# Memory retrieval from the transposed queries: row-tiled matmuls on [M | z], the division after the matmul, and a new order of the attention steps

## The chip, the core and the metric

One core of a Trainium2 chip runs the whole kernel. The metric is the device time of one execution in microseconds; lower is better. The engines are named as in the profile: PE is TensorE's matmul stream and PEld its weight loads, DVE is VectorE, ACT is ScalarE, POOL is GpSimd, SP issues most of the DMAs.

## The reference

Attention with a compressed memory over B = 4 batches, H = 8 heads, S = 576 tokens, D = 64, followed by two feed-forward layers on the 2304 x 512 result:

```python
scores = scale * np.matmul(q, k.transpose(0, 1, 3, 2))      # causal, softmax -> a
local = np.matmul(a, v)
q_p = phi(q)                                                # elu(q) + 1
mem_ret = np.einsum('bhsd,bhde->bhse', q_p, M_prev)
mem_norm = np.einsum('bhsd,bhd->bhs', q_p, z_prev)[..., None] + 1e-06
g = 1.0 / (1.0 + np.exp(-beta))[None, :, None, None]
attn = g * mem_ret / mem_norm + (1 - g) * local
...
h = x @ w_in;  y = (h * np.cos(h)) @ w_out                  # first layer
r = np.maximum(y @ w2_in, 0);  out = (r * r) @ w2_out       # second layer
```

The `moe_` and `moe2_` weights come as 64-bit floats and are turned into fp32, and from there into a high and a low fp32r part, on the chip.

## The kernel before

**Attention.** The work is cut into 16 units, one for each batch and pair of heads. The two heads of a pair stand on partitions 0 to 63 and 64 to 127 of the transposed operands, so a matmul with 64 rows of one head can run beside that of the other. For a unit u the steps are: `S0` to `S3` (scores, fp32, into the PSUM pool `ps_s` of two buffers), `R0` to `R3` (DVE: mask, scale and row minimum out of PSUM), `E0` to `E3` (ACT: exp with row sums), `Ns0`, `Ns1` (DVE: reciprocals with the gate), `Np0` to `Np3` (POOL: normalise the probabilities), `PT0` to `PT6` (PE transposes of the probabilities into the pool `ps_t` of two buffers), `V0` to `V6` (copies of these into SBUF, by ACT or DVE as the string `pt` says), `PV0` to `PV4` (probabilities times v, into the one accumulator `O_t`), `mem` (memory part added into `O_t`), `X` (ACT copies `O_t` out, a DMA stores it as a slice of `xT`).

**Memory retrieval before.** `q1` to `q3` make phi(q) from q in row form (`qr`, a load of its own, 320 KB per unit). `q4` (POOL) multiplies it by z, broadcast over 128 partitions by a DMA (`zb`); `q5` (DVE) sums it over d and takes the reciprocal with the gate; `q6` (POOL) multiplies phi(q) by that; `qpT` transposes the product on PE and `qpV` copies it out on ACT; `mem` multiplies it with a block-diagonal M (128 x 128, `mbd`), 512 and 64 columns wide, into `O_t`.

**Conversion of weights.** `c1` to `c9` carry one weight tile per unit through the 64-bit conversion: `c1` absolute value (ACT), `c2` clamp (DVE here), `c3`, `c4`, `c6` (DVE), `c5` (ACT), then for the first 8 units the high and low split (`c8` ACT, `c9` POOL), for the last 8 a store.

**Order.** `CFG['order']` is a list of step/offset pairs, run once for each u from -2 on; `S1/2` in round u is the step S1 of unit u+2. Each engine runs its steps of the list in this order (the `_Pinned` wrapper chains them), so one late step holds all behind it on its engine. SP issues the DMAs in order too: in a round the loads of unit u+2 (line 720 on), then `xT`, the v load after `PV3`, and the next weight tile. Buffers: `qk` (transposed q and k, 640 KB) and `qr` two each, `vr` three, raw weights two.

**End of attention.** `CFG['fill']` puts the first three steps of the feed-forward part (`l` = its matmuls, `a` to `g` = its elementwise chain) into the slots of units that no longer exist. The feed-forward part itself (`moe`) is not pinned: the tile framework places its instructions where its own schedule finds room, inside the last rounds of attention too. In the trace its lines bear their own numbers (L157 to L169, L256), those of attention L47 or L44.

Of the kernel before, what the change touches and what calls it, by code (L numbers as in the profile page):

```python
# [32 lines left out]
class _Pinned:  # L33
# [23 lines left out]
    S0/1 c5/1 R1/1 PT0/0 PT1/0 X/-2 E1/1 q5/0 S2/1 PV0/-1 R0/1 R2/1 V1/0 PV2/-1 PV1/-1 q1/1 V0/0  # L57
    c1/0 PV4/-1 q6/0 PV3/-1 PT2/0 E0/1 q2/1 PT4/0 c2/0 Ns0/1 S3/1 mem/-1 c3/0 c4/0 Np2/0 V2/0 R3/1
    PT3/0 qpT/0 Np0/1 q3/1 E2/1 V4/0 c6/0 PT6/0 V3/0 PT5/0 qpV/0 Np1/1 V5/0 V6/0 S1/2 E3/1 q4/1
    Ns1/1 c8/0 c9/0 Np3/1  # L60
""",
       'pt': 'AAAAADD',
       'norm': 'PPPP',
       'qpt': 'A',
# [20 lines left out]
def kernel(  # L85
# [14 lines left out]
    nc = tc.nc  # L100
# [48 lines left out]
    def c_steps(raw, clamp=None, rest=None):  # L149
# [6 lines left out]
        return af, [  # L156
            lambda: act.activation(out=af, in_=hi.bitcast(F32), func=AF.Abs),  # L157
            lambda: (clamp or pool).tensor_scalar(
                out=af, in0=af, scalar1=MAG_MAX, scalar2=MAG_MIN, op0=ALU.min, op1=ALU.max
            ),  # L160
            lambda: dve.tensor_scalar(
                out=a, in0=a, scalar1=3, scalar2=0x3FFFFFF8,
                op0=ALU.logical_shift_left, op1=ALU.bitwise_and,
            ),
            lambda: dve.scalar_tensor_tensor(  # L165
                out=b, in0=hi, scalar=-0x40000000, in1=a, op0=ALU.bitwise_and, op1=ALU.bitwise_or
            ),
            lambda: act.activation(out=r, in_=lo.bitcast(U32), func=AF.Copy, scale=2.0 ** -29),
            lambda: dve.tensor_tensor(out=a, in0=b, in1=r, op=ALU.add),  # L169
        ]  # L170
# [153 lines left out]
    def attention(ctx):  # L324
# [14 lines left out]
        mbd = [ac.tile([128, NP, 128], F32, name=f"mbd{i}") for i in range(2)]  # L339
# [11 lines left out]
        def load(u, first=False):  # L351
            b, p = divmod(u, NP)
            t = ae.tile([128, 2 * S + 128], F32, tag="qk", name="qk")
            if first:
                nc.scalar.dma_start(out=t[:, S:2 * S], in_=qk[b, p, :, S:2 * S])
                nc.sync.dma_start(out=t[:, 0:S], in_=qk[b, p, :, 0:S])
                nc.scalar.dma_start(out=t[:, 2 * S:], in_=qk[b, p, :, 2 * S:])
            else:
                nc.sync.dma_start(out=t, in_=qk[b, p])
            raw["qk", u] = t  # L360
            t = ae.tile([128, NKT, 2, D], F32, tag="qr", name="qr")
            nc.sync.dma_start(out=t, in_=qrow[b, p])
            raw["q", u] = t
            t = ae.tile([128, 2, D], F32, tag="zb", name="zb", bufs=3)
            nc.sync.dma_start(
                out=t.rearrange("p h d -> p (h d)"),
                in_=z_prev[b:b + 1, 2 * p:2 * p + 2].rearrange("o h d -> o (h d)").partition_broadcast(128),
            )
            raw["z", u] = t
# [7 lines left out]
        def load_mem(b):  # L377
            m = mbd[b % 2]
            for h in range(2):
                nc.sync.dma_start(  # L380
                    out=m[h * 64:(h + 1) * 64, :, h * 64:(h + 1) * 64],
                    in_=M_prev[b].rearrange("(p two) d e -> two d p e", two=2)[h],
                )

        qp_t = {}

        ee = {}

        def q1(u):
            qr = raw["q", u].rearrange("p t h d -> p (t h d)")  # L390
            ee[u] = ae.tile([128, NKT * 2, D], F32, tag="e", name="e", bufs=1)
            ef = ee[u].rearrange("p a d -> p (a d)")
            dve.tensor_scalar(out=ef, in0=qr, scalar1=0.0, scalar2=None, op0=ALU.min)

        def q2(u):
            ef = ee[u].rearrange("p a d -> p (a d)")
            act.activation(out=ef, in_=ef, func=AF.Exp)

        def q3(u):
            qr = raw["q", u].rearrange("p t h d -> p (t h d)")  # L400
            qp_t[u] = ae.tile([128, NKT * 2, D], F32, tag="qp", name="qp")
            dve.scalar_tensor_tensor(
                out=qp_t[u].rearrange("p a d -> p (a d)"), in0=qr, scalar=0.0,
                in1=ee[u].rearrange("p a d -> p (a d)"), op0=ALU.max, op1=ALU.add,
            )

        def q4(u):
            zz = raw["z", u].rearrange("p h d -> p (h d)")
            pool.tensor_tensor(
                out=ee[u].rearrange("p (t h) d -> p t (h d)", h=2),  # L410
                in0=qp_t[u].rearrange("p (t h) d -> p t (h d)", h=2),
                in1=zz.unsqueeze(1).to_broadcast([128, NKT, 2 * D]),
                op=ALU.mult,
            )
# [15 lines left out]
        def q6(u):  # L430
            mnf = mns.pop(u).rearrange("p t h -> p (t h)")
            pool.tensor_tensor(
                out=qp_t[u], in0=qp_t[u], in1=mnf.unsqueeze(2).to_broadcast([128, NKT * 2, D]),
                op=ALU.mult,
            )

        qpT = {}

        def emit_qpT(u):
            qp = qp_t.pop(u)  # L440
            ps = ps_s.tile([128, 2, 512], F32, tag="s", name="qps").rearrange("p a b -> p (a b)")
            for t in range(NKT):
                w = KW[t]
                pe.transpose(
                    out=ps[:, t * 128:t * 128 + w],
                    in_=qp[0:w, 2 * t:2 * t + 2, :].rearrange("p h d -> p (h d)"),
                    identity=ident[0:w, 0:w],
                )
            qpT[u] = ps
# [145 lines left out]
        def emit_mem(u):  # L595
            b, p = divmod(u, NP)
            for a, e in ((0, 512), (512, S)):
                pe.matmul(
                    out=O_t[u][:, a:e],
                    lhsT=mbd[b % 2][:, p, :],  # L600
                    rhs=qpT[u][:, a:e],
                    start=False,
                    stop=True,
                    skip_group_check=True,
                )
# [56 lines left out]
        for t in mbd:  # L662
# [24 lines left out]
        def conv_load(n):  # L687
            if todo and 0 <= n < NU:
                what, kd, f = todo.pop()
                tiles[n] = [what, kd, f, *c_steps(c_load(wsrc[kd, 1], kd, f), dve, a2)]  # L690

        def conv(n, x):
            what, kd, f, wf, ops = tiles[n][:5]
            if x <= 6:
                if x == 5 and n == 0:
                    return
                if x == 2 and n == 0:
# [15 lines left out]
            "q1": q1, "q2": q2, "q3": q3, "q4": q4, "q5": q5, "q6": q6,  # L713
            "qpT": emit_qpT, "qpV": emit_qpV, "mem": emit_mem, "X": emit_X,
# [3 lines left out]
        XL, xraws = CFG["xl"], []  # L718
        for u in range(first, end):
# [10 lines left out]
            for t, d in program:  # L730
# [6 lines left out]
                if 0 <= u + d < NU:  # L737
                    if t == "Ns0" and u + d == 0:
                        gates()
# [180 lines left out]
_INS = ['M_prev', 'z_prev', 'beta', 'moe_w_in', 'moe_w_out', 'moe2_w_in', 'moe2_w_out']  # L920
# [3 lines left out]
def _layout(np, q, k, v):  # L924
# [16 lines left out]
    return {"qk": qk, "qrow": rows(q), "vrow": rows(v)}  # L941
# [28 lines left out]
```

## Time and profile before

| | |
|---|---|
| median of 3 runs | 1047.77 us (1046.26 to 1050.31) |
| the profiled execution | 1047.47 us, span 1045.7 us |
| busy over the span | PE 96%, PEld 76%, DVE 58%, ACT 54%, POOL 28% |
| chain that ended last, by engine | PE 71%, DVE 10%, DMA 8%, ACT 7% |

The busy shares mix two parts: attention, up to about 228 us, in which all engines work, and the feed-forward part, in which PE does nearly everything. Attention has to be read by itself.

### The profile page before, as it was taken

The page shows a single profiled execution, that of the slowest core. Times are in us where ns is not written, and L with a number is a line of the kernel's source. Part 1 is how long each engine was busy: PE and PEld are TensorE (multiplying, and loading weights), DVE is VectorE, ACT ScalarE, POOL GpSimd, SP SyncE. Part 2 cuts the span into 40 slices and gives each one's busy share as a digit, 9 for nine tenths or more (in the row PEclk, how much of TensorE's full clock was granted, in tenths as well). Part 3 has the DMA queues.
Part 4 walks back from the last instruction along what each step waited for, and adds up shares of the span by engine and source line. Part 5 has one row for each costly group of instructions (what it writes and reads, how often), then busy time and mean ns, then how long its engine had stood idle before and what let it go on. Part 6 is the DMA issues. An engine that isn't in the chain of part 4 may idle for free.

```text
span 1045.7 us, 14485 instructions
## 1 busy us (share of the span) xinstructions
PE 1005.4 (96%) x5200; PEld 796.0 (76%) x5200; DVE 603.2 (58%) x1235; ACT 567.6 (54%) x1152; POOL 288.9 (28%) x306
## 2 busy tenths in 40 slices
PE   6999999879899999999999999999999999999998
PEld 4666666657687778788998778788888888888887
DVE  5999999648777878555555589623222322322232
ACT  5999999757776766445556667423222322322222
POOL 5999888637432110000003544300000000000000
PEclk8999999989999999999999999999999999999999
DMA  7565666144425664100103324201100200000010
GB/s 213 178 209 195 217 210 216 66 134 140 141 81 155 188 208 155 41 1 20 61 21 110 112 82 135 87 1 41 41 1 1 71 1 1 21 31 1 0 42 21
DMA packets 56873, 95.33 MB, mean 91 GB/s; under 512 B 8032, under 2 KB 29920, under 8 KB 56800
## 3 DMA queue, kind: packets, MB, share of 16 engines
q1 hardware_dynamic: 56224, 93.90, 28.0%
q8 instruction: 41, 0.67, 0.3%
q10 hardware_dynamic: 576, 0.50, 0.1%
q14 instruction: 32, 0.26, 0.1%
HBM read 72.88 MB, written 21.50 MB: 90 GB/s over the span
## 4 chain that ended last, share of the span: by engine, by line
PE 71%; DVE 10%; DMA 8%; ACT 7%; issue 3%; POOL 2%; SPq 0%; POOLq 0%; DVEq 0%; ACTq 0%
PE a L772 29%; PE h L256 28%; PE o L47 5%; PE ptps L47 3%; PE sps L47 3%; DMA wraw<-in_moe_w_out_dram 2%; DVE wa L169 1%; DVE wb L165 1%; DMA wf<-ws2in 1%; DMA xraw<-xT 1%; DVE gf L289 1%; DMA ws2out<-wa 1%; PE h L47 1%; DMA wf<-ws2out 1%; DMA ws2in<-wa 1%
## 5 line engine op out<-in xcount | busy, mean ns | idle before, releaser
L256 PE MATMUL h<-xh,winh 128*128 128x512 f32 (+1 forms) x628 | 234.0, 373 | 3.6 <-DVE gf L302 1.7
L256 PE MATMUL h<-xl,winh 128*128 128x512 f32 (+1 forms) x628 | 233.6, 372 | 0.0
L256 PE MATMUL h<-xh,winl 128*128 128x512 f32 (+1 forms) x628 | 233.1, 371 | 0.0
L314 DVE TENSOR_TENSOR gl<-gf,gh 128x512 fp32r<-128x512 f32 (+1 forms) x156 | 104.5, 670 | 130.0 <-ACT gh L307 129.8
L307 ACT ACTIVATE gh<-gf 128x512 fp32r<-128x512 f32 (+1 forms) x158 | 92.2, 584 | 113.6 <-PE a L772 96.1
L256 PEld LDWEIGHTS h<-xh,winh 128*128 128x128 f32 x628 | 118.2, 188 | 28.6 <-DVE gf L302 3.3
L256 PEld LDWEIGHTS h<-xh,winl 128*128 128x128 f32 x628 | 118.3, 188 | 22.4
L256 PEld LDWEIGHTS h<-xl,winh 128*128 128x128 f32 x628 | 118.2, 188 | 22.4
L285 DVE TENSOR_TENSOR gf<-gf 128x512 f32<-128x512 f32 (+1 forms) x80 | 51.9, 653 | 134.7 <-ACT gf L277 134.5
L277 ACT ACTIVATE gf<-h 128x512 f32<-128x512 f32 (+1 forms) x80 | 43.9, 554 | 152.0 <-PE h L256 151.1
L772 PE MATMUL a<-gl,wouth 128*128 128x512 f32 (+1 forms) x320 | 118.0, 375 | 0.6 <-DVE gl L314 0.5
L772 PE MATMUL a<-gh,woutl 128*128 128x512 f32 (+1 forms) x320 | 117.8, 374 | 0.0
L772 PE MATMUL a<-woutl,gh 128*128 128x512 f32 x288 | 112.9, 392 | 0.0
L772 PE MATMUL a<-wouth,gl 128*128 128x512 f32 x288 | 112.9, 392 | 0.0
L47 POOL TENSOR_SCALAR P<-P,sm 128x512 f32<-128x512 f32 (+3 forms) x128 | 97.4, 779 | 13.1 <-DVE sm L47 11.9
L772 PE MATMUL a<-wouth,gh 128*128 128x512 f32 x288 | 99.1, 393 | 1.1 <-ACT gh L307 1.1
L772 PE MATMUL a<-gh,wouth 128*128 128x512 f32 (+1 forms) x320 | 85.9, 375 | 8.2 <-ACT gh L307 7.3
L302 DVE TENSOR_TENSOR gf<-h,gf 128x512 f32<-128x512 f32 (+1 forms) x78 | 49.4, 634 | 60.4 <-PE h L256 43.7
L772 PEld LDWEIGHTS a<-gh,wouth 128*128 128x128 f32 x320 | 56.4, 188 | 22.8 <-ACT gh L307 11.0
L275 ACT ACTIVATE ki<-h 128x512 int32<-128x512 f32 (+1 forms) x77 | 42.2, 548 | 57.9 <-DVE gf L302 49.0
L47 PE MATMUL sps<-qk 64*128 64x384 f32 (+4 forms) x320 | 63.1, 455 | 8.7 <-DMA qk<-in_qk_dram 4.6
L772 PEld LDWEIGHTS a<-gl,wouth 128*128 128x128 f32 x320 | 61.0, 191 | 12.4 <-DVE gl L314 1.4
(113 smaller groups left out, 1631.9 us busy)
## 6 DMA issues: line engine op xcount, KB each, us to landing
wraw<-in_moe_w_in_dram SPq DMA_DIRECT2D x32, 512.0 KB, 3.9
wraw<-in_moe_w_out_dram SPq DMA_DIRECT2D x32, 512.0 KB, 3.7
qk<-in_qk_dram SPq DMA_DIRECT2D x15, 640.0 KB, 5.1
qr<-in_qrow_dram SPq DMA_DIRECT2D x16, 320.0 KB, 4.6
vr<-in_vrow_dram SPq DMA_DIRECT2D x16, 320.0 KB, 2.9
xT<-x SPq DMA_DIRECT2D x16, 288.0 KB, 3.1
out_dram<-ob SPq DMA_DIRECT2D x17, 256.0 KB, 2.3
x1T<-ob SPq DMA_DIRECT2D x16, 256.0 KB, 2.6
```

The costliest lines, as they stand in the source:

```text
L47: made = call(*args, **kwargs)
L165: lambda: dve.scalar_tensor_tensor(out=b, in0=hi, scalar=-0x40000000, in1=a, op0=ALU.bitwise_and, op1=ALU.bitwise_or),
L169: lambda: dve.tensor_tensor(out=a, in0=b, in1=r, op=ALU.add),
L256: pe.matmul(out=h[:, 0:n], lhsT=lt[:, kk * 128:(kk + 1) * 128], rhs=rt[:, 0:n], start=(kk == 0 and x == 0), stop=(kk == KD - 1 and x == 2),)
L275: act.activation(out=kis[s], in_=hs[s], func=AF.Copy, scale=1.0 / TWO_PI)
L277: act.activation(out=rs[s], in_=hs[s], func=AF.Relu)
L285: dve.tensor_tensor(out=rs[s], in0=rs[s], in1=rs[s], op=ALU.mult)
L289: dve.scalar_tensor_tensor(out=rs[s], in0=kis[s], scalar=-C2, in1=rs[s], op0=ALU.mult, op1=ALU.add)
L302: dve.tensor_tensor(out=rs[s], in0=hs[s], in1=rs[s], op=ALU.mult)
L307: act.activation(out=gh, in_=rs[s], func=AF.Copy)
L314: eng.tensor_tensor(out=gl, in0=rs[s], in1=gs[s].bitcast(F32), op=ALU.subtract)
L772: nc.tensor.matmul(out=o, lhsT=lt, rhs=rt, start=((p, j, f) in opens and x == 0), stop=((p, j, f) in closes and x == 2),)
```

## The change

The memory part starts from the transposed q, which is already there in `qk`. `q1` to `q3` work on 576 columns of it and write phi(q) transposed into `qpb`. A new step `qm` multiplies, for each of the five blocks of 128 tokens and each head, 64 rows of phi(q) (stationary) with [M | z] of that head (64 x 65, moving): the product has the 64 retrieved columns and the norm in column 65, both heads in their own PSUM bank. `q4` (DVE) takes norm, gate and reciprocal from PSUM, `q5` (DVE) multiplies the retrieved columns by it on their way to SBUF (`mr`), and `mem` becomes five accumulating transposes of `mr` into `O_t`. The loads `qr` and `zb` go; a small load `zcol` comes. `q4` and `q6` on POOL, `qpT` and `qpV` go. `c1` moves from ACT to DVE, `c2` from DVE to POOL, `V3` from ACT to DVE. The order is new; `mem` now runs two rounds late, and for the last two units `mem` and `X` follow the last `PV` at once. The first M and v loads come later.

```diff
-    S0/1 c5/1 R1/1 PT0/0 PT1/0 X/-2 E1/1 q5/0 S2/1 PV0/-1 R0/1 R2/1 V1/0 PV2/-1 PV1/-1 q1/1 V0/0
-    c1/0 PV4/-1 q6/0 PV3/-1 PT2/0 E0/1 q2/1 PT4/0 c2/0 Ns0/1 S3/1 mem/-1 c3/0 c4/0 Np2/0 V2/0 R3/1
-    PT3/0 qpT/0 Np0/1 q3/1 E2/1 V4/0 c6/0 PT6/0 V3/0 PT5/0 qpV/0 Np1/1 V5/0 V6/0 S1/2 E3/1 q4/1
-    Ns1/1 c8/0 c9/0 Np3/1
+    V6/-1 Np3/0 c5/1 c2/0 c8/-1 S0/1 S2/1 q1/1 PT1/0 R0/1 PT0/0 R2/1 E1/1 q2/1 Np2/0 S3/1 V1/0 PT2/0
+    V0/0 c3/0 mem/-2 PT3/0 c4/0 R3/1 qm/0 E0/1 S1/2 V3/0 V2/0 E3/1 Ns0/1 PT4/0 X/-2 PT5/0 c6/0 PV0/-1
+    PV3/-1 q3/1 q4/0 V5/0 q5/0 c9/-1 E2/1 V4/0 Np1/1 Np0/1 Ns1/1 c1/1 PV2/-1 R1/2 PV4/-1 PV1/-1 PT6/0
-       'pt': 'AAAAADD',
+       'pt': 'AAADADD',
+       'abs': 'D',
+       'clamp': 'P',
...
+            dve.tensor_scalar(out=a, in0=hi, scalar1=0x7FFFFFFF, scalar2=None, op0=ALU.bitwise_and)
...
-        mbd = [ac.tile([128, NP, 128], F32, name=f"mbd{i}") for i in range(2)]
+        mbd = [ac.tile([128, NP, 65], F32, name=f"mbd{i}") for i in range(2)]
+        qpb = [a2.tile([128, 640], F32, name=f"qp{i}", bufs=1) for i in range(2)]
...
-            nc.sync.dma_start(out=t, in_=qrow[b, p])
...
+            nc.sync.dma_start(out=m[:, :, 64:65], in_=zcol[b])
...
+        def qm(u):
+            b, p = divmod(u, NP)
+            ps = mem_ps[u] = ps_s.tile([128, 2, 512], F32, tag="s", name="qps")
+            for t in range(NKT):
+                for h in range(2):
+                    r = slice(64 * h, 64 * h + 64)
+                    pe.matmul(
+                        out=ps[:, h, 65 * t:65 * t + 65],
+                        lhsT=qpb[u % 2][r, 128 * t:128 * t + 128],
+                        rhs=mbd[b % 2][r, p, :],
+                        start=True, stop=True,
+                    )
...
+        def q5(u):
+            mr[u] = a2.tile([128, NKT, 2, D], F32, tag="mr", name="mr")
+            dve.tensor_tensor(
+                out=mr[u].rearrange("p t h d -> p h t d"),
+                in0=mem_view(u)[:, :, :, 0:64],
+                in1=mns.pop(u).rearrange("p t h -> p h t").unsqueeze(3).to_broadcast([128, 2, NKT, D]),
                 op=ALU.mult,
             )
...
         def emit_mem(u):
-            for a, e in ((0, 512), (512, S)):
+            src = mr.pop(u)
+            for t in range(NKT):
+                w = KW[t]
                 pe.matmul(
-                    lhsT=mbd[b % 2][:, p, :],
-                    rhs=qpT[u][:, a:e],
+                    out=O_t[u][:, 128 * t:128 * t + w],
+                    lhsT=src[0:w, t].rearrange("p h d -> p (h d)"),
+                    rhs=ident[0:w, 0:w],
                     start=False,
                     stop=True,
+                    is_transpose=True,
...
-                    if t == "PV3" and u + d + 3 < NU:
-                        load_v(u + d + 3)
+                    if (t, d) == last_pv:
+                        if u + d + 3 < NU:
+                            load_v(u + d + 3)
+                        if u + d >= NU - 2:
+                            emit_mem(u + d)
+                            emit_X(u + d)
             if u == -1:
-                load_v(2)
+                load_mem(0)
+                for x in range(3):
+                    load_v(x)
```

## Rows read from the trace of the kernel before

**Rows 1.** Stages: start:end, us, busy (instructions) of PE, PEld, DVE, ACT, POOL, clock, DMA share, GB/s.
```profile
0.00:28.89 28.89, 18.17 (x88) 12.49 (x88) 16.64 (x61) 17.34 (x49) 16.17 (x30) 0.88 0.72 222
28.89:183.19 154.30, 150.78 (x1170) 101.87 (x1171) 142.03 (x446) 146.62 (x377) 137.07 (x152) 1.00 0.61 202
40.00:75.00 35.00, 34.95 (x275) 23.73 (x272) 32.32 (x103) 34.28 (x88) 33.23 (x37) 1.00 0.55 190
183.19:227.71 44.52, 35.80 (x237) 24.44 (x236) 25.86 (x62) 26.12 (x55) 19.10 (x22) 0.88 0.28 92
227.71:430.00 202.29, 193.45 (x810) 153.29 (x810) 158.45 (x249) 140.57 (x239) 61.21 (x58) 0.98 0.48 149
...
215.50:222.30 6.80, 3.23 (x18) 1.61 (x20) 4.51 (x5) 3.29 (x6) 2.66 (x3) 0.50 0.27 88
```

**Rows 2.** The chain that ended last, one round: start us, us, what.
```profile
55.70 3.18 PE o L47 x36
...
60.88 1.03 PE o L47 x4
61.90 0.45 PE ptps L47 x4
62.35 0.64 PE qps L47 x5
...
65.39 1.02 PE ptps L47 x8
66.41 0.85 PE sps L47 x8
```

**Rows 3.** The same chain, before the first regular round.
```profile
10.16 9.04 DMA wraw<-in_moe_w_out_dram
```

**Rows 4.** The same chain, 98 to 153 us.
```profile
111.74 1.35 DVE xl L47
...
134.10 4.42 DMA qr<-in_qrow_dram
```

**Rows 5.** Timeline of PE at the end of attention; in brackets idle time before, its releaser.
```profile
197.43 0.44 PE L47 MATMUL ptps<-ident,P 128*128 128x128 f32 x2 [2.83 <-ACT PT L47]
...
213.27 0.55 PE L47 MATMUL ptps<-ident,Pl 128*128 128x128 f32 x3 [1.02 <-ACT PT L47]
...
219.07 4.82 PE L47 MATMUL o<-PT,vr 128*64 128x512 f32 x36 [4.87 <-ACT x L47]
```

**Rows 6.** Timeline of PEld at the start of S2, stretch 54.77 to 54.90 us.
```profile
54.78 0.30 PEld L47 LDWEIGHTS sps<-qk 64*128 64x128 f32 x4 [0.16 <-DVE mx L47]
```

**Rows 7.** Groups by form, 100 to 400 us: shapes xcount | busy us, mean ns | idle.
```profile
L47 PEld LDWEIGHTS sps<-qk 64*128 64x128 f32 x120 | 10.3, 186 | 8.3 <-DVE mx L47 5.0 <-issue 1.0 <-DVE wa L47 0.2
```

**Rows 8.** Groups by form, DVE, five rounds from 40.46 to 98.36 us.
```profile
L47 DVE SCALAR_TENSOR_TENSOR wb<-wraw,wa 128x512 int32<-128x512 int32 x5 | 5.3, 1056 | 0.2
...
L47 DVE TENSOR_REDUCE mn<-e 128x10 f32<-128x640 f32 x5 | 4.1, 815 | 0.0
...
L47 DVE CUSTOM_DVE_ANT_0 Pl<-sps,maskl 128x576 f32<-128x576 f32 x5 | 3.8, 758 | 0.9 <-PE sps L47 0.6
...
L47 DVE TENSOR_SCALAR wa<-wa 128x512 f32<-128x512 f32 x5 | 2.1, 420 | 0.0
```

**Rows 9.** Groups by form, ACT and POOL, the five rounds of rows 8.
```profile
L47 ACT ACTIVATE PT<-ptps 128x512 f32<-128x512 f32 x25 | 14.2, 590 | 1.0 <-PE ptps L47 0.4
...
L47 ACT ACTIVATE wa<-wraw 128x512 f32<-128x512 f32 x5 | 3.5, 695 | 0.0
...
L47 ACT ACTIVATE qpT<-qps 128x576 f32<-128x576 f32 x5 | 3.3, 652 | 0.2
...
L47 POOL TENSOR_TENSOR e<-qp,zb 128x640 f32<-128x640 f32 x6 | 9.2, 1541 | 0.0
L47 POOL TENSOR_TENSOR qp<-qp,mn 128x640 f32<-128x640 f32 x5 | 6.3, 1262 | 2.5 <-DVE mn L47 2.5
```

**Rows 10.** DMA issues from 45 to 182 us: KB each, median us to landing.
```profile
qk<-in_qk_dram SPq DMA_DIRECT2D x11, 640.0 KB, 5.0
```

More of the change, by code (lines that the diff above doesn't have):

```diff
@@ L147, in c_load, with c_abs, c_steps @@
         return raw
-    def c_steps(raw, clamp=None, rest=None):
+    def c_abs(eng, a, af, hi):
+        if eng == "A":
+            act.activation(out=af, in_=hi.bitcast(F32), func=AF.Abs)
+        else:
+            dve.tensor_scalar(out=a, in0=hi, scalar1=0x7FFFFFFF, scalar2=None, op0=ALU.bitwise_and)
+    def c_steps(raw, clamp=None, rest=None, mag="A"):
         a = wr.tile([128, DM], I32, tag="wa", name="wa")
@@ L156, in c_steps @@
         return af, [
[L157 removed]
+            lambda: c_abs(mag, a, af, hi),
             lambda: (clamp or pool).tensor_scalar(
@@ L378, in load_mem @@
             m = mbd[b % 2]
[L379 to L387, printed above, removed]
+            nc.sync.dma_start(
+                out=m[:, :, 0:64], in_=M_prev[b].rearrange("(p two) d e -> (two d) p e", two=2)
+            )
+            nc.sync.dma_start(out=m[:, :, 64:65], in_=zcol[b])
@@ L389, in q1 @@
+        ee, mem_ps, mr = {}, {}, {}
         def q1(u):
[L390 to L393, printed above, removed]
+            ee[u] = ae.tile([128, S], F32, tag="e", name="e", bufs=1)
+            dve.tensor_scalar(
+                out=ee[u], in0=raw["qk", u][:, 0:S], scalar1=0.0, scalar2=None, op0=ALU.min
+            )
@@ L407, in q4 @@
-        def q4(u):
[L408 to L412, printed above, removed]
+                out=qpb[u % 2][:, 0:S], in0=raw["qk", u][:, 0:S], scalar=0.0,
+                in1=ee.pop(u), op0=ALU.max, op1=ALU.add,
+            )
+        def qm(u):
[9 more added lines that the diff above has]
+                        start=True, stop=True,
+                    )
@@ new lines, in attention, with mem_view @@
+        mns = {}
+        def mem_view(u):
+            return mem_ps[u][:, :, 0:65 * NKT].rearrange("p h (t c) -> p h t c", c=65)
+        def q4(u):
+            p = u % NP
+            mns[u] = mn = a2.tile([128, NKT, 2], F32, tag="mn", name="mn")
+            dve.scalar_tensor_tensor(
+                out=mn.rearrange("p t h -> p h t"),
+                in0=mem_view(u)[:, :, :, 64], scalar=1e-6,
+                in1=ig[:, 2 * p:2 * p + 2].unsqueeze(2).to_broadcast([128, 2, NKT]),
+                op0=ALU.add, op1=ALU.mult,
+            )
+            mnf = mn.rearrange("p t h -> p (t h)")
+            dve.reciprocal(out=mnf, in_=mnf)
@@ L430, in q6 @@
[L430 to L449, printed above, removed]
@@ L661, in attention @@
             )
-        for t in mbd:
+        for t in (t[:, S:] for t in qpb):
             pool.memset(t, 0.0)
@@ L689, in conv_load @@
                 what, kd, f = todo.pop()
-                tiles[n] = [what, kd, f, *c_steps(c_load(wsrc[kd, 1], kd, f), dve, a2)]
+                tiles[n] = [what, kd, f, *c_steps(
+                    c_load(wsrc[kd, 1], kd, f), dve if CFG["clamp"] == "D" else pool, a2, CFG["abs"]
+                )]
         def conv(n, x):
@@ L696, in conv @@
                     return
-                if x == 2 and n == 0:
+                if x == 3 and n == 0:
                     ops[4]()
@@ L712, in attention @@
             "V": emit_V, "PV": emit_PV, "c": conv,
-            "q1": q1, "q2": q2, "q3": q3, "q4": q4, "q5": q5, "q6": q6,
-            "qpT": emit_qpT, "qpV": emit_qpV, "mem": emit_mem, "X": emit_X,
+            "q1": q1, "q2": q2, "q3": q3, "q4": q4, "q5": q5, "qm": qm, "mem": emit_mem, "X": emit_X,
         }
@@ L736, in attention @@
                             g_do(x, n)
-                if 0 <= u + d < NU:
-                    if t == "Ns0" and u + d == 0:
-                        gates()
+                if 0 <= u + d < NU and not (t in ("mem", "X") and u >= NU):
+                    if t in ("Ns0", "Ns1", "q4") and not gated:
+                        gated.append(gates())
                     if t in emit:
@@ L952 @@
     arrays, args = {}, []
-    given = _layout(_np, *(_np.asarray(inputs[n]) for n in "qkv"))
+    given = _layout(_np, *(_np.asarray(inputs[n]) for n in ("q", "k", "v", "z_prev")))
     for name in _INS:
```

50 lines of the change are left out of this document (8 added, 42 removed), and 11 rows, old and new, of the table CFG.

## Prediction

> **What bounds the kernel now.** Read the stages first [rows 1]. The change acts only up to 227.71 us, where attention ends. In the regular rounds (40 to 75 us) all four engines are nearly full: PE 34.95 of 35 us, ACT 34.28, POOL 33.23, DVE 32.32. Shares alone do not say who sets the pace, so the chain that ended last comes next [rows 2]: from 55.70 to 67.26 us, one PV to the next, it is PE without a break, S, PT, PV, mem and qpT one after another. A round is 11.56 us because PE's instructions take 11.56 us. ACT and POOL are close behind, but relief for them buys nothing here by itself.
>
> PE is not the pace everywhere. Three places have other chains. Before the first regular round, which begins at 28.89 us, the chain lies on a load [rows 3]. The 13 rounds from 28.89 to 183.19 us take 154.30 us [rows 1], 4.0 more than 13 times 11.56; the extra lies in rounds in which DVE also splits the x tiles (`xl`) and a q load is waited for [rows 4]. The end of attention takes 44.52 us, with PE idle for 2.83, 1.02 and 4.87 us [rows 5].
>
> **PE in a regular round.** Out go `mem` in its old form, 1.03 us, and the `qpT` transposes, 0.64 us [rows 2]. In come five transposes into `O_t`; they have the shapes of `qpT`, so 0.64 us again. In comes `qm`: 10 matmuls of 64 rows. An fp32 matmul is two instructions, each with its own weight load (S2, four matmuls, shows 8 [rows 2]), so 20 loads of 128 columns and 20 streams of 65 columns. Four such loads, for both heads, take 0.30 us in S2 [rows 6]; one lasts 0.186 [rows 7], so the second pair started 0.11 us after the first, and the two heads of a pair load side by side. Ten pairs at 0.11 are 1.1 us. The streams hide under the loads: S2 moves 256 + 128 columns of a head pair, twice, in 0.85 us, 1.1 ns per column, so 65 columns cost at most 0.07. The new order also splits the row-tiled and the full-array blocks once more. Eight transposes in a block of their own between score blocks take 1.02 us, four inside a full-array block 0.45 [rows 2]; so a block's entry and exit cost 0.12. Sum: -1.03 - 0.64 + 0.64 + 1.1 + 0.12 = +0.2, a round of 11.7 us. Bounds: if the streams and not the loads set the pace, `qm` is 0.7 and the round 11.3; if the 20 loads run one by one, `qm` is 2.2 and the round 12.8. I take the pairs, since the nearest row, of the same shape, shows them.
>
> [...]
>
> **DVE in a regular round.** It has 32.32/35 of 11.56 = 10.7 us of work [rows 1]. Out: the reduction, 0.82, and the clamp, 0.42 [rows 8]. In: `q5`, 640 elements out of PSUM, and `V3`, 512; the 576-element pass out of PSUM takes 0.76 [rows 8], so 0.84 and 0.67. In too: the absolute value, 512 integers at a step of two words, between the contiguous 0.42 and the 1.06 of the two-input step on the same strided operand [rows 8]; I take 0.5, since it has one input. `q1` and `q3` lose a tenth of their columns, about 0.1. The two small steps on the norm stay, now out of PSUM. Sum 11.2, under PE's 11.7; with the upper bound 11.8, and then DVE is level with PE.
>
> **ACT and POOL.** ACT loses 0.65 (`qpV`), 0.70 (`c1`) and 0.59 (`V3`) [rows 9], 1.9 us of about 11.3. POOL loses 1.54 and 1.26 [rows 9] and gains a clamp of 512 elements, 0.9 by the mean of its instructions (137.07 us in 152 [rows 1]). Each gets some 2 us of slack per round. PE covers all that, so it is costed at nothing; without that cover it would be worth what they held the chain, which is within the 4.0 us above.
>
> **Waits in the new order.** I walk a round with S0 at 0, by the durations of the chain: S0 and S2 to 1.7, two PT to 2.6, S3 to 3.6, PT2, `mem`, PT3 to 5.4, `qm` to 6.5, S1 to 7.3, PT4 and PT5 to 8.1, PV to 11.2, PT6 to 11.7. DVE starts with V6 behind PT6, then q1 and R0, which ends at about 2.3; S3 needs its buffer at 2.6. That is DVE's closest wait. The closest of all is a load. `v` of unit u+2 needs the buffer that the last PV frees, at 11.2, and stands on SP's queue ahead of `qk` of the next round, which so is issued at about 0.2 and lands 5.0 us later [rows 10]: at 5.2, for S1 at 6.5. Before, S1 stood at the end of the round. Behind S1 on PE stand PT4, PT5 and PV, on DVE R1. I allow 1 us in all for the rounds in which x tiles, stores or M loads share the queues.
>
> **The three other places.** *Rounds with x tiles:* DVE has 11.2 and up to 1.35 for `xl` [rows 4] against 11.7, say 0.5 too much in four rounds, 2 us, where 4.0 was lost before; the q load that was waited for (4.42 us, [rows 4]) no longer exists. *Start:* the chain waits 9.04 us for the second raw weight tile [rows 3]. Two q loads and three z broadcasts, 832 KB, no longer stand before it, and M and v come later. At 222 GB/s [rows 1] 832 KB are 3.7 us; DVE's own work is next in line, so I take 3 (bounds 0 and 5). [...] Now `X` of the unit before follows its PV at once. 4.87 + 1.64 = 6.5; I take 6, since the other two idle stretches, behind PT copies on ACT, may stay or grow (bounds 0 and 10, the latter if they go too).
>
> **Sum.** Against the profiled execution (1047.5 us; span 1045.7 and 1.8 around it; the median of the runs is 1047.8, the same within 0.3): start -3; 13 rounds 13 x 11.7 + 2 + 1 = 155.1 for 154.3, +0.8; end -6. What follows is PE work (193.45 of 202.29 us busy, [rows 1]) and moves along. 1047.5 - 8.2 = 1039.3 us. The gain is at the ends; the regular rounds pay for it slightly.
>
> **Rivals.**
> - *The qk load comes late (slower).* S1 has 1.3 us of slack. If `qk` lands after 7.5 us instead of 5.0, every round waits 1.2 us: 13 x 1.2 = 15.6, 1055 us. It turns the result from 0.63 us of wait per round on (8.2/13), a landing after 6.9. For it: `v`, `qk` and the x tiles follow one another on one queue. Against: q rows and z no longer share it, and the 5.0 was measured with them there. Chance 0.12.
> - *Weight loads of the two heads run one by one (slower).* The round is 12.8: 13 x 1.1 = 14.3 more, 1053.6 us. Rows 6 speak against it. Chance 0.04.
> - *The ends stay as they are (no change).* Feed-forward steps still stand on ACT ahead of PT copies, or new ones on DVE, now the fullest engine beside PE; start -2, end 0: 1046.3 us. Chance 0.20.
> - *`qm` runs at the pace of its streams (faster).* The round is 11.3: 5.2 less, 1034 us. Chance 0.07.
>
> **How the numbers follow.** My forecast has 0.57. Its own range: 1034 (start 5, end 9) to 1045 (DVE level with PE, 0.1 per round, start 2, end 3). The range given, 1030 to 1053, takes in the faster rival with a good end and the unchanged one, and reaches toward the late load. A change within 0.5% (5.2 us) can't be told from none on this kernel. Faster than 1042.5: most of my forecast, 0.52, the stream rival's 0.07 and a little of the third, 0.02: 0.61. Slower than 1053: 0.12 of the two slower rivals' 0.16, and 0.02 for more. Same: the rest, 0.25.
>
> **What would show it.** Right: the chain in regular rounds still PE, a round of 11.6 to 11.8 us, `qm` near 1.1 us in 20 instructions; the first regular round some 3 us earlier; no wait of the last PV for `X`, granted clock 1.00 there; ACT and POOL near 80% in regular rounds. Wrong: PE waiting for `qk` before S1, a round bound by DVE (R0 late for S3), `qm` at 0.7 or 2.2 us, or idle time of PE at the end as long as before.

## The result and the profile after

The changed kernel takes 1037.8 us (median of 4 runs, 1036.67 to 1039.37) where the kernel before takes 1048.4 beside it (1046.26 to 1050.31): a ratio of 0.9892, 95% interval 0.9874 to 0.9911. The profiled execution took 1039.37 us, 8.1 less than that of before. It is the slowest of the four, so its stages account for 8.1 us, where the medians differ by 10.6; a second profile of the same kernel (r1 below) shows the rest. Read the stages first, cut as in [rows 1], with the start of the 13 rounds counted back from their end (windows; columns as there, the granted clock third from the end):

```profile
0.00:28.30 28.30, 20.57 (x109) 13.98 (x109) 18.82 (x71) 18.30 (x50) 14.08 (x30) 0.88 0.61 193
28.30:181.68 153.38, 153.38 (x1371) 108.49 (x1371) 140.15 (x459) 125.24 (x338) 99.37 (x140) 0.99 0.53 168
40.00:75.00 35.00, 35.00 (x318) 24.68 (x316) 31.57 (x105) 28.82 (x78) 23.40 (x33) 1.00 0.52 159
181.68:218.15 36.47, 33.27 (x271) 24.08 (x270) 23.64 (x55) 19.76 (x42) 11.71 (x18) 1.00 0.34 114
218.15:420.40 202.25, 191.56 (x799) 152.36 (x800) 161.32 (x247) 138.88 (x239) 61.12 (x58) 0.97 0.47 149
...
14.90:21.70 6.80, 5.74 (x23) 4.64 (x24) 5.27 (x21) 5.10 (x12) 5.14 (x8) 0.50 0.23 86
```

| stage | before, us | after, us | difference | predicted |
|---|---|---|---|---|
| start, to the first regular round | 28.89 | 28.30 | -0.6 | -3 |
| 13 rounds | 154.30 | 153.38 | -0.9 | +0.8 |
| end of attention | 44.52 | 36.47 | -8.05 | -6 |
| feed-forward part, to the end of the span | 818.0 | 819.45 | +1.4 | 0 |

The end of attention carries the gain. In the 13 rounds PE is busy 153.38 of 153.38 us, so the trace shows no wait of it there; ACT has fallen from 34.28 to 28.82 of 35 us and POOL from 33.23 to 23.40. One round in the chain that ended last, to be held against [rows 2] (start us, us, what):

```profile
60.08 3.18 PE o L47 x36
63.26 0.48 PE ptps L47 x3
63.73 1.71 PE sps L47 x12
65.45 1.02 PE ptps L47 x8
66.47 0.97 PE sps L47 x4
67.44 0.44 PE ptps L47 x4
67.88 0.64 PE o L47 x5
68.52 0.59 PE ptps L47 x4
69.11 1.26 PE qps L47 x20
70.37 0.70 PE sps L47 x4
71.07 0.81 PE ptps L47 x6
```

From one PV to the next it is 11.80 us (the sum of these rows is 11.80), and the twelve rounds from the first PV (36.48 us) to the last regular one (178.03) take that each, those with x tiles too. The first of the 13 is another case. Its `S0` ran at 26.52, the cut at 28.30 falls on its `S2`, and from there to its PV it takes 8.2 us, as long as a regular round takes from `S0`. Cut at that `S0`, the start would be 2.3 us shorter than before and the 13 rounds 0.7 longer. Only the sum of the two, -1.5 us, does not hang on the cut. Before, an ordinary round was shorter (11.56), but the 13 took 4.0 more than 13 of them. `qm` is the row `qps` x20, `mem` the row `o` x5.

At the start (timeline of PE, in brackets the idle time before and its releaser) the load of [rows 3] is gone from the chain, and other things took its place:

```profile
15.96 1.65 PE L47 MATMUL sps<-qk 64*128 64x256 f32 x8 [4.15 <-DVE mx L47]
17.55 1.97 PE L47 MATMUL ptps<-ident,P 128*128 128x128 f32 x8
19.31 2.12 PE L47 MATMUL sps<-qk 128*128 128x288 f32 x4
...
28.30 1.48 PE L47 MATMUL sps<-qk 64*128 64x256 f32 x8 [0.66 <-DVE mx L47]
```

PE stands idle for 4.15 us behind R1 on DVE. From 14.9 to 21.7 us the granted clock is 0.50 (last row of the stages), and S2, eight transposes and S3 take about twice what they take in a regular round (in the chain 1.65 us for 0.85, 1.90 for 1.02 and 1.92 for 0.97). Behind three shorter idle stretches (0.47, 0.23 and 0.66 us between 25.3 and 28.3) the clock is 0.50 again from 28.5 to 31.9 us, so the first round loses time to it too (its S2 takes 1.48 us for 0.85). The start of before ran at the same mean clock, 0.88 in the first line of both stage views. At the end (same view) the three idle stretches of [rows 5], 2.83, 1.02 and 4.87 us, have become these:

```profile
203.44 0.44 PE L47 MATMUL ptps<-ident,P 128*128 128x128 f32 x2 [0.47 <-ACT PT L47]
...
205.03 3.25 PE L47 MATMUL o<-PT,vr 128*64 128x512 f32 x36 [0.72 <-ACT x L47]
...
211.01 1.53 PE L47 MATMUL o<-PT,vr 128*64 128x512 f32 x16 [1.46 <-ACT x L47]
```

The last PV starts at a granted clock of 1.00 (211.0 to 212.5 us) and takes 1.53 us for 16 instructions, where [rows 5] have 4.82 for 36.

What ACT did is the second half of that story. In the kernel before, its timeline at the end of attention has two waits that the prediction did not read:

```profile
196.24 0.66 ACT L168 ACTIVATE wc<-wraw 128x512 int32<-128x512 uint32 x1 [2.76 <-DMA wraw<-in_moe_w_in_dram]
...
211.58 0.67 ACT L168 ACTIVATE wc<-wraw 128x512 int32<-128x512 uint32 x1 [2.32 <-DMA wraw<-in_moe_w_out_dram]
```

Line 168 is a conversion step of the feed-forward part, placed by the framework among attention's last copies; it waits for its raw weight tile, and `PT` and `qpT` copies stand behind it. In the timeline of the changed kernel the same step (now line 172) finds its tile there:

```profile
190.06 0.68 ACT L172 ACTIVATE wc<-wraw 128x512 int32<-128x512 uint32 x1
...
203.28 0.68 ACT L172 ACTIVATE wc<-wraw 128x512 int32<-128x512 uint32 x1
```

### The profile page after: what moved, and what is told of

The parts are those of the page before. It is cut to its first block, busy times and chain, and to the rows that moved or that the text cites. A ratio compares the mean times of both kernels' runs of the same rounds, so it can differ in the third digit from the quotient of the medians.

```text
span 1037.6 us, 14910 instructions
## 1 busy us (share of the span) xinstructions
PE 1007.8 (97%) x5456; PEld 804.6 (78%) x5456; DVE 604.8 (58%) x1251; ACT 539.9 (52%) x1104; POOL 241.3 (23%) x290
## 4 chain that ended last, share of the span: by engine, by line
PE 74%; DVE 10%; DMA 6%; ACT 5%; issue 3%; POOL 2%; SPq 0%; DVEq 0%; ACTq 0%; POOLq 0%
PE h L260 28%; PE a L760 28%; PE o L47 5%; PE sps L47 5%; PE ptps L47 5%; DVE wb L169 2%; PE qps L47 2%; DVE wa L173 1%; DMA ws2in<-wa 1%; DMA wf<-ws2in 1%; DVE gl L318 1%; DMA xraw<-xT 1%; DVE gf L293 1%; DVE wa L165 1%; DMA wf<-ws2out 1%
## 5 line engine op out<-in xcount | busy, mean ns | idle before, releaser
L47 POOL TENSOR_SCALAR P<-P,sm 128x384 f32<-128x384 f32 (+3 forms) x128 | 84.8, 680 | 71.1 <-DVE sm L47 69.7
L47 ACT ACTIVATE P<-P,mx 128x384 f32<-128x384 f32 (+3 forms) x127 | 69.7, 552 | 11.1 <-DVE mx L47 11.0
```

## The experiments

Twelve runs. Ratios are to the kernel before, with 95% intervals; the end of attention is that of the last matmul into `O_t` in the timeline of the profiled execution (for before 227.87, 0.16 later than in the chain by which [rows 1] are cut), the rest what follows it in the span. The last three columns are those of one execution each; those of r2, r3, r4 and r9 lie 1.7 to 4.1 us above the median of their kernel.

| run | median us | ratio | ordinary round | attention ends | rest |
|---|---|---|---|---|---|
| before | 1048.2 | 1 | 11.56 | 227.9 | 817.9 |
| r1 changed, again | 1037.05 | 0.9893 [0.9874, 0.9912] | 11.80 | 216.9 | 818.3 |
| r2 late end | 1036.69 | 0.9883 [0.9863, 0.9903] | 11.80 | 218.0 | 818.7 |
| r3 warm start | 1037.8 | 0.9894 [0.9875, 0.9913] | 11.80 | 217.7 | 820.1 |
| r4 full mem | 1034.14 | 0.9862 [0.9842, 0.9883] | 11.55 | 214.3 | 820.8 |
| r5 before, early X | 1043.49 | 0.9953 [0.9936, 0.9971] | 11.56 | 222.6 | 819.7 |
| r6 half columns | 1038.28 | 0.9910 [0.9889, 0.9930] | 11.80 | 218.4 | 817.2 |
| r7 old engines | 1043.0 | 0.9950 [0.9934, 0.9965] | 13.03, then 11.95 | 224.5 | 816.7 |
| r8 block diagonal | 1038.5 | 0.9903 [0.9878, 0.9927] | 11.80 | 219.6 | 818.5 |
| r9 before, own raw | 1045.49 | 0.9969 [0.9946, 0.9992] | 11.56 | 225.0 | 822.8 |
| r10 before, raw and X | 1044.31 | 0.9960 [0.9940, 0.9980] | 11.56 | 218.7 | 824.0 |
| r11 clamp on DVE | 1038.92 | 0.9904 [0.9866, 0.9941] | 11.95 | 218.9 | 817.4 |
| r12 combined | 1032.05 | 0.9841 [0.9808, 0.9873] | 11.55 | 213.5 | 816.7 |

### The changed kernel again

> The changed kernel once more, so that the variants beside it have their measure on the same chip. Both theories expect the ratio measured before, 0.987 to 0.991, some 1037 to 1039 us.

It came out so. Its profile differs from the first one in the start, with the first regular round at 27.05 us (1.8 earlier than before) and less time at a granted clock of 0.50 (17 to 20 us), and in what follows attention (818.3 us for 819.5). Its stages, -1.8, -0.9, -8.05 and +0.3 us against before, add up to -10.5, what the medians differ by. So the start's gain is 0.6 to 1.8 us, not one number.

### What ends the wait for X: r2 and r5

In r2 the special case for the last two units is taken out:

```diff
-                if 0 <= u + d < NU and not (t in ("mem", "X") and u >= NU):
+                if 0 <= u + d < NU:
...
-                        if u + d >= NU - 2:
-                            emit_mem(u + d)
-                            emit_X(u + d)
```

> The changed kernel, but mem and X of the last two units stay at their own places in the order, two rounds late, behind the feed-forward steps that fill the empty rounds. Theory 1 (the gain at the end comes from the early X): the last PV waits for X again, 5 to 6 us of the 8 us gained at the end are lost, 1043 to 1045 us, and the granted clock falls to 0.5 near the last PV. Theory 2 (the gain at the end comes from ACT and POOL, which have 2 us less work per round, so that X finds ACT free wherever it stands): at most 2 us lost, 1038 to 1040 us.

Nothing was lost: the stage is 36.50 us instead of 36.47. The chain at the end of r2, where the changed kernel has 210.42 and 211.01:

```profile
210.31 0.55 ACT x L47
...
210.90 1.53 PE o L47 x16
```

X of unit 14 runs at the same time wherever it is issued, behind the same feed-forward steps on ACT. Theory 1 falls for the new order. Theory 2 is right in that at most 2 us are lost; r7 below tests its cause. In r5 the kernel before gets the early X alone:

```diff
+                    if t == "mem" and u + d >= NU - 2:
+                        emit_X(u + d)
```

> The kernel before, with one thing alone of the change: X of the last two units is issued right behind their mem, one round earlier than before, ahead of the feed-forward steps on ACT. Theory 1 (the early X carries the gain at the end): the last PV no longer waits 4.87 us nor runs at half clock, 5 to 6.5 us faster than before, 1041 to 1043 us. Theory 2 (ACT is too full in the old order and X is late all the same): less than 2 us.

Here it is worth 4.8 us, and attention ends 5.25 us earlier (222.62 for 227.87); 1.1 of these lie ahead of the end of attention, whose `S0` starts at 182.08 us for 183.19. PE no longer waits for X, as theory 1 said, but the other half of theory 1 did not come: PE stands idle for 2.25 us a little earlier (209.7 to 211.9), the granted clock is 0.50 from 213.0 to 216.3, and the last PV takes longer than a regular one:

```profile
214.48 4.15 PE L47 MATMUL o<-PT,vr 128*64 128x512 f32 x36
```

In the old order X stood a round late at the cost that the prediction read; in the new order that position no longer matters.

### The wait for the raw weight tile: r9 and r10

```diff
+        def own(n):
+            return a2.tile([128, 2 * DM], I32, tag="wrawx", name="wrawx", bufs=1) if n == NU - 1 else None
...
-            t = a2.tile([128, S], F32, tag="qpT", name="qpT")
+            t = a2.tile([128, S], F32, tag="qpT", name="qpT", bufs=1)
```

> The kernel before, with the raw tile of attention's last weight tile in a buffer of its own (and one buffer for qpT instead of two, to make room), so that the first two raw tiles of the feed-forward part need not wait for it. In the profile of before, ACT stands still for 2.76 and 2.32 us at the end of attention, at the unpinned conversion step on line 168 that waits for a raw weight tile, with PT and qpT copies queued behind it. Theory 3 (this wait is what the end of before loses and the changed kernel does not have): the waits of line 168 for wraw vanish, the end gets 3 to 5 us shorter, 1043 to 1045 us. Theory 1 (X behind feed-forward steps on ACT is what counts): PE still waits for X before the last PV, at most 1.5 us faster, 1046.5 us or more.

> The kernel before with both: the raw tile of its own and the early X of the last two units. If both waits together are the end's gain of the change (8 us on the profiled executions), the end falls from 44.5 to 36 to 38 us, 1040 to 1041 us. If they are one and the same wait, so that one of them gone is enough, the time stays at the 1043.5 us of the early X alone.

Timelines of ACT and of PE in r9:

```profile
184.53 0.67 ACT L168 ACTIVATE wc<-wraw 128x512 int32<-128x512 uint32 x1 [1.78 <-DMA wraw<-in_moe_w_in_dram]
...
207.15 0.67 ACT L168 ACTIVATE wc<-wraw 128x512 int32<-128x512 uint32 x1 [0.58 <-DVE wa L169]
```

```profile
215.22 5.79 PE L47 MATMUL o<-PT,vr 128*64 128x512 f32 x36 [4.86 <-ACT x L47]
```

The second wait for a tile is gone, the first one shorter (1.78 for 2.76), and the last PV starts at 215.22 instead of 219.07; it still waits 4.86 us for X, and the granted clock is 0.50 from 214 to 220 us. Both theories had a part: attention ends 2.84 us earlier, and the median is 2.8 us lower, with an interval that only just leaves out no change. (The profiled execution is the slowest of ten, so its 822.8 us of rest is not typical.) With both edits (r10) attention ends at 218.73, 9.1 us earlier than before, close to where the changed kernel ends it (216.9 to 218.1). Counted from the `S0` that begins the end of attention, that stage is 4.1 us shorter in r5, 3.0 in r9 and 9.1 in r10 (35.6 us, where 36 to 38 were expected). So these are two separate waits, and the two edits together give 2 us more than their sum. At least a part of that is the clock: with one wait left the last PV ran in part at a granted clock of 0.50 (4.15 us in r5, 5.79 in r9), with none (1.00 throughout the end) it takes what a regular one takes:

```profile
211.51 3.25 PE L47 MATMUL o<-PT,vr 128*64 128x512 f32 x36
```

The time as a whole did not follow in r10, 1044.31 us and not 1040 to 1041: its feed-forward part takes 824.0 us, 6.1 more than before. The timeline of PE shows two long idle stretches there, where the two longest of before are 3.31 and 1.54 us:

```profile
240.38 0.79 PE L256 MATMUL h<-xh,winh 128*128 128x512 f32 x1 [4.54 <-DVE gf L281]
...
311.65 2.07 PE L777 MATMUL a<-gh,wouth 128*128 128x512 f32 x4 [2.65 <-ACT gh L307]
```

An earlier end of attention is not simply carried through: PE then waits for the elementwise chain of the next feed-forward steps. The framework places that part anew for each kernel, and it comes out between 816.7 and 824.0 us (table), of which a part is the spread between executions (1.2 us between the two profiles of the changed kernel). What decides the rest was not tried.

### The start: r3

```diff
+                    if t == "S2" and u == 0:
+                        wps2 = ps_t.tile([128, 4, 128], F32, tag="t", name="wps2")
+                        for _ in range(20):
+                            pe.matmul(out=wps2[:, 0, :], lhsT=ones, rhs=ones, start=True, stop=True)
```

> The changed kernel with 20 matmuls of 128 x 128 that compute nothing, put into PE's idle stretch (4.15 us, 11.8 to 15.96 us) ahead of S2 of unit 1. Theory 1 (the start's gain was lost to the granted clock of 0.5 that follows this idle stretch): S2, the PT and S3 behind it run at full clock (0.85, 1.02 and 0.97 us for 1.65, 1.90 and 1.92), the first regular round starts 2 to 3 us earlier, 1035 to 1036 us. Theory 2 (DVE, not PE, sets the start's pace; a faster PE only waits longer for R): the first regular round starts within 0.7 us of 28.3, no change within 1 us.

Stages of r3, and one row of its PE timeline at the end:

```profile
0.00:25.43 25.43, 21.85 (x147) 16.50 (x149) 17.54 (x66) 17.46 (x49) 12.97 (x29) 1.00 0.64 205
...
178.79:217.65 38.86, 34.82 (x271) 25.25 (x270) 23.63 (x55) 19.87 (x42) 11.69 (x18) 0.96 0.33 107
```

```profile
208.97 2.12 PE L47 MATMUL o<-PT,vr 128*64 128x512 f32 x16 [2.31 <-ACT x L47]
```

Theory 1 is right about the place: with PE kept busy the granted clock is 1.00 throughout the start, and the first regular round begins at 25.43 us, 1.6 to 2.9 earlier than in the two profiles of the changed kernel. The time stayed the same by the median; two of the six executions came at 1035.3 and 1035.8 us, where theory 1 had put it, and the profiled one is among the longest (1039.48). In it the end takes 38.86 us instead of 36.47. The rounds end 2.9 us sooner, but X comes only 2.0 sooner, because ACT's conversion step ahead of it (line 149) waits 0.74 us for a store of converted weights. The chain of r3 has that store:

```profile
202.91 4.27 DMA ws1out<-wa
```

In the changed kernel the same store takes 2.0 us and nobody waits for it; why it took longer here is open. So PE waits 2.31 us for X instead of 1.46, and then the granted clock is 0.50 there, from 210 to 213 us: the store and the clock took the gain of the start.

### PE's round: r4, r6 and r8

In r4 the last transpose of `mem` gets 128 rows:

```diff
-                w = KW[t]
+                w = 128
```

> The changed kernel with all five mem transposes on 128 rows, the last one too (its 64 extra rows and columns land in a part of O that nobody reads). In the changed kernel that transpose of 64 rows is entered after 203 ns, where the others follow at 109, and it splits the full-array block. Theory 1 (the change of the tile's rows costs the time): mem and the transposes behind it get 0.2 to 0.25 us shorter, a round 11.55 to 11.6 instead of 11.80, 13 to 16 rounds, 3 to 4 us less, 1034 to 1035 us. Theory 2 (the time is a cost of the last transpose itself, or comes back at the next entry): round 11.75 to 11.80, no change within 0.7 us.

Four rows of its chain, to be held against 67.44 to 69.11 of the changed kernel:

```profile
89.43 0.44 PE ptps L47 x4
89.87 0.55 PE o L47 x5
90.41 0.44 PE ptps L47 x4
90.85 1.26 PE qps L47 x20
```

`mem` 0.55 for 0.64, the four transposes behind it 0.44 for 0.59: 0.24 us per round, 11.55 in all, and 2.9 us in the median. Theory 1 holds: here less work on one tile costs more than full work. Of the 0.24 us, 0.09 lie in `mem`, whose last tile it is, and 0.15 in the group behind it; what PE does at these two places no run here shows.

In r6 `qm` streams half the columns (the other 32 retrieved columns are left out):

```diff
-                        out=ps[:, h, 65 * t:65 * t + 65],
+                        out=ps[:, h, 65 * t + 32:65 * t + 65],
...
-                        rhs=mbd[b % 2][r, p, :],
+                        rhs=mbd[b % 2][r, p, 32:65],
```

> The changed kernel with 33 moving columns instead of 65 in every matmul of qm; the other 32 retrieved columns are left out, and q5 writes the same 32 twice. Theory 1 (qm's time is that of its 20 weight loads, two heads side by side): qm stays at 1.2 to 1.26 us and the round at 11.8. Theory 2 (the streams of 65 columns set the pace): qm falls by a third or more, to 0.85 us or less, the round to 11.4, 5 us less.

In r8 it is done on the full array:

```diff
-                for h in range(2):
-                    r = slice(64 * h, 64 * h + 64)
-                    pe.matmul(
-                        out=ps[:, h, 65 * t:65 * t + 65],
-                        lhsT=qpb[u % 2][r, 128 * t:128 * t + 128],
-                        rhs=mbd[b % 2][r, p, :],
...
+                pe.matmul(
+                    out=ps[:, t // 3, 130 * (t % 3):130 * (t % 3) + 130],
+                    lhsT=qpb[u % 2][:, 128 * t:128 * t + 128],
+                    rhs=mbd[b % 2][:, p, :],
```

> The changed kernel with qm on the full array: five matmuls of 128 rows with a block-diagonal [M z 0 0; 0 0 M z] of 130 columns, 10 weight loads and 10 streams instead of 20 of 64 rows in pairs. q4 and q5 take two instructions each more on DVE. Theory 1 (a load takes its 128 columns whatever its rows, and pairs of 64 rows go side by side, so ten pairs cost what ten full loads cost): qm 1.1 to 1.3 us, the round 11.7 to 11.9, no change within 1.5 us. Theory 2 (the row-tiled pairs are the gain of the change): qm 2 us or more, the round 12.5, 10 us slower.

The chain of r6, then that of r8:

```profile
91.63 1.24 PE qps L47 x20
```

```profile
93.60 1.12 PE qps L47 x10
94.72 0.84 PE sps L47 x4
```

Half the columns leave `qm` at 1.24 us (1.26 with all of them): its time does not go with its columns, which points to its 20 weight loads. Each of them lasts 0.187 us in the changed kernel (40 to 75 us), as do those of 64 rows in the scores there, where one of 128 rows lasts 0.189; so 20 in 1.26 us overlap. Ten full loads take 1.12 us, ten pairs of 64 rows 1.26; what `qm` saves, S1 behind it pays (0.84 for 0.70), so that both sums are 1.96 and the round 11.80. Row tiling neither gains nor loses here. (In the rounds with x tiles both kernels take 12.01 us; in both `q5` is two instructions on DVE, which is the likely reason.)

### The engines of the moved steps: r7 and r11

```diff
-       'pt': 'AAADADD',
-       'abs': 'D',
-       'clamp': 'P',
+       'pt': 'AAAAADD',
+       'abs': 'A',
+       'clamp': 'D',
```

> The changed kernel with the three moved steps back on their old engines: absolute value on ACT, clamp on DVE, V3 on ACT. ACT gets 1.9 us per round more (about 11.3 of 11.8), DVE some 1.5 less, POOL 0.6 less. Theory 1 (PE sets the regular round, the moves buy nothing there): the round stays 11.80, the end of attention loses at most 1 us, no change within 1.5 us. Theory 2 (the slack of ACT is what lets PE run without a break): PE waits for ACT in rounds with x tiles and at the end, 3 us or more slower, above 1041 us.

6 us slower, in time nearer to theory 2, but not by its mechanism: PE does not wait for ACT, and the end of attention takes 36.88 us (36.47 in the changed kernel). With that, theory 2 of r2 falls in its cause too as far as ACT goes; POOL stays as light here as in the changed kernel, so its part is not tested. Five rounds take 13.03 us. Timelines of DVE, of POOL and of PE in one of them:

```profile
77.69 1.52 DVE L47 TENSOR_SCALAR e<-qk 128x576 f32<-128x576 f32 x1
```

```profile
77.43 1.46 POOL L47 TENSOR_TENSOR winl<-wa,winh 128x512 fp32r<-128x512 f32 x1
```

```profile
80.48 1.24 PE L47 MATMUL sps<-qk 128*128 128x288 f32 x4 [0.97 <-DVE mx L47]
```

`q1` on DVE takes 1.52 us where its median is 0.45; it began 0.26 us after POOL's subtraction `winl` and ended 0.3 after it, and so in each of the five rounds. R0 stands behind it, and S3 on PE waits 0.97 us for R0. To see whether the clamp alone does that, r11 moves only it:

```diff
-       'clamp': 'P',
+       'clamp': 'D',
```

> The changed kernel with only the clamp back on DVE. With all three steps on their old engines five rounds took 13.03 us, and in each q1 on DVE took 1.52 us instead of 0.45, beside POOL's subtraction winl; R0 behind it was late for S3. Theory 1 (the clamp ahead of q1 moves q1 into POOL's winl): five or six rounds of 13 us again, 5 us or more slower than the changed kernel, 1042 us or more. Theory 2 (it is the fuller ACT): no round over 12 us, within 1.5 us of the changed kernel.

It does not. Theory 1 falls in that form: no round is over 12 us, and the median is 1.9 us above that of r1 (the intervals overlap), near the 1.5 of theory 2; theory 2's own cause, the fuller ACT, is neither shown nor excluded by this run. Chain, POOL and DVE of r11:

```profile
77.63 1.13 PE sps L47 x4
```

```profile
75.46 1.93 POOL L47 TENSOR_TENSOR winl<-wa,winh 128x512 fp32r<-128x512 f32 x1
```

```profile
75.47 0.41 DVE L47 TENSOR_SCALAR wa<-wa 128x512 f32<-128x512 f32 x1
75.81 0.45 DVE L47 TENSOR_SCALAR e<-qk 128x576 f32<-128x576 f32 x1
```

This time `winl` was the long one (1.93 us for 1.28, alike in five rounds), and nobody waits for it. What the clamp costs is plainer: R0 comes 0.34 us later, S3 takes 1.13 us instead of 0.97, and every round is 11.95; 13 x 0.15 = 2.0 us. So DVE's slack before S3 was 0.34 - 0.15, about 0.2 us. In r7 `winl` begins 0.26 us before q1, here 0.35 us, and the one time q1 is the long one (1.52 us), the other time `winl`. What decides it was not tried by itself.

### The combination: r12

r4 and r3 together, with 8 more such matmuls ahead of the last PV:

```diff
+                    if (t == "S2" and u == 0) or (t == "PV0" and u + d == NU - 1):
+                        wps2 = ps_t.tile([128, 4, 128], F32, tag="t", name="wps2")
+                        for _ in range(20 if t == "S2" else 8):
```

> The changed kernel with mem's last transpose on 128 rows, the 20 matmuls that compute nothing ahead of S2 at the start, and 8 more of them ahead of the last PV, where the granted clock fell to 0.5 when the start came earlier. Theory 1 (the gain at the start is kept when the last PV does not fall to half clock): rounds of 11.55, first PV 2 us earlier than in the changed kernel, end of attention near 212 us, 1031 to 1033 us. Theory 2 (what is gained ahead of the feed-forward part is given back in it): 1034 us, as with the full transposes alone.

Timeline of PE ahead of the last PV, and the last two stages of attention:

```profile
204.10 2.05 PE L47 MATMUL wps<-ones 128*128 128x128 f32 x16
206.41 1.53 PE L47 MATMUL o<-PT,vr 128*64 128x512 f32 x16 [0.25 <-ACT x L47]
```

```profile
26.39:176.60 150.21, 149.70 (x1375) 107.26 (x1371) 140.32 (x463) 125.59 (x338) 100.23 (x141) 1.00 0.54 173
176.60:213.45 36.85, 34.52 (x286) 25.89 (x286) 23.42 (x55) 19.83 (x42) 11.66 (x18) 1.00 0.34 113
```

1032.05 us, 5.0 below r1, and theory 1's number (attention's end is 1.5 us later than it said). The clock is 1.00 up to the end of attention, the last PV runs in 1.53 us for its first 16 instructions, and attention ends at 213.45 us. The slow store of r3 is there too (4.11 us); what r12 saves against r3 at the end, 36.85 us for 38.86, goes with the clock. It beats the changed kernel (0.9841 [0.9808, 0.9873] against 0.9893 [0.9874, 0.9912]); against r4 alone its interval overlaps (0.9842 to 0.9883), so the part of the filling matmuls rests on the profiles.

## Why the prediction was right, and where it was not

**The total** was 1.5 us off by the median. On the profiled execution the sum was 8.2 against 8.1 us, and that is luck: its four terms were off by 2.4, 1.7, 2.1 and 1.4 us, two of them each way, and cancel.

**The round** was right in its mechanism: PE, without a break, 11.80 for 11.7. The sum said 11.56 + 0.2, and 0.24 were measured: `qm` takes 1.26 us, entry included, where 1.1 and 0.12 were taken, and `mem` 0.64 as taken. What the step did not see is that the 64-row tile in it costs 0.24 of that round (r4). Half the columns leave `qm` at 1.24 us (r6), so its streams do not set its pace, and its 20 loads of 64 rows take 1.26 where ten of 128 take 1.12 (r8); the rivals of the stream's pace (0.7) and of loads one by one (2.2) fall with them.

**The rounds with x tiles** were put at 3 us too much (x tiles 2, loads 1) and cost nothing. DVE has 31.57/35 x 11.80 = 10.6 us per round and not 11.2 (the terms as listed add up to 11.35). The absolute value is dearer than taken (0.63 for 0.5), but `wb` fell from 1.06 [rows 8] to 0.69, the gate step `sm` on five columns from 0.51 to 0.16, and q1 and q3 run at 0.45 and 0.75 (0.49 and 0.95 before). This is the term of the sum that was mis-sized.

**The late qk load** did not come: PE is never idle in the 13 rounds, so no load holds it. The walk had SP's queue the wrong way round: its timeline has the `qk` load at 47.85 us, ahead of the v load at 51.51 and not behind it, and S1 needs it at 58.58.

**"PE covers all that, so it is costed at nothing"** holds for POOL and ACT as long as DVE is not touched; DVE's closest wait, R0 for S3, was named with 0.3 us of slack and has 0.2. By r11, 0.34 us on DVE costs 0.15 per round; by r7 the three moves together are worth 6 us. They are no side matter of the change. Of the two signs named for the slack, "near 80%", ACT shows 82% and POOL 67%.

**The start** failed at "DVE's own work is next in line, so I take 3": the load went, DVE did come next, with 4.15 us of idle PE, and 0.6 to 1.8 us were gained. The step left out what follows such stretches here, the granted clock of 0.50 from 14.9 to 21.7 and from 28.5 to 31.9 us. With the clock at 1.00 (r3) the gain is 28.89 - 25.43 = 3.5 us, so 1.6 to 2.9 us were lost to it, and the 3 was a fair size for a start that keeps PE busy.

**The end** was right in size (8.05 for 6) and wrong in its cause. The 1.64 in its sum is what the last PV of before takes above a regular one, 4.82 [rows 5] less 3.18 [rows 2]; in r10, with neither wait, that PV takes 3.25. The step "X of the unit before follows its PV at once" is refuted by r2: without it nothing is lost. In the old order two waits bore on the end, X's place (4.1 us of this stage by r5) and ACT standing still for raw weight tiles (3.0 by r9); both edits in the old kernel end attention close to where the change does (r10). That the change has neither wait is seen in the profile. Which part of it removes them, the order, the fill table, or the missing `qpV` on ACT, is not separated; the engine moves do not (r7's end is 36.88 us).

**The rest** "moves along": nearly. It grew by 1.4 us (0.3 in r1), in r10 by 6.1.

## What to carry to other kernels

Read the engine that copies and evacuates for waits on loads before giving a late step's delay to its place in the order: the wait that PE shows names only the last one in the queue. An odd small tile within a block of full ones cost more here than doing it full size (0.24 us per round, r4). A gain early in a kernel reaches its end only if no later wait takes it back: r3 lost it to a store that ACT waited for and to the clock behind the wait, r12 kept the clock up and the gain with it.

## What the runs showed of the hardware that was not expected

**Some instructions of DVE and POOL took longer where the two engines overlapped.** These are q1 with 1.52 us for 0.45 beside `winl` (r7), `winl` with 1.93 for 1.28 (r11), and, argued only from the traces, `wb`. In the kernel before it took 1.06 us in a round in which POOL works beside it (70.56 to 73.42 us); in the changed kernel it takes 0.69, and POOL stands idle beside it (66.59 to 70.32). In r7, with `c1` and `c2` on their old engines again, it is 0.69 as well. In r7 `winl` came 0.26 us before q1, and q1 ends at 79.21, 0.3 us after the end of `winl` at 78.89. In r11 `winl` begins 0.01 us before a step of DVE and is the long one, while q1, which begins 0.35 us after it, takes its usual 0.45. Not every overlap did this: in the changed kernel `winl` takes 1.28 us beside R0 (from 77.11 us). What decides it no run shows.

**The clock fell after PE's idle stretches in several places, not in all.** Near the last PV it fell behind 4.87 us [rows 5], 4.86 (r9), 2.31 (r3) and 2.25 (r5) of idle time, and not behind 1.61 (r2), 1.46 (changed kernel), 1.27 (r10) or 0.25 (r12, with matmuls that compute nothing in the gap). The length of the last stretch alone does not tell it: at 28.5 us of the changed kernel it fell behind 0.66 us, with 0.47 and 0.23 shortly before, and in r1 it stayed at 1.00 behind 1.50 ahead of the first regular round. At the start 4.15 us of idle time came with a granted clock of 0.50, and the same stretch filled with matmuls kept it at 1.00.
